# K and Q of the first half batch in fp32 by SyncE's queue, in a fused attention and feed-forward kernel

## The chip, the cores and the metric

The kernel runs on one core of one Trainium2 chip. The core has five engines that work side by side and wait for each other by semaphores: TensorE (PE, matrix products), VectorE (DVE), ScalarE (ACT), GpSimd (POOL) and SyncE (SP). Sixteen DMA engines move data between HBM and the on-chip memory; transfers are issued from the queues of SyncE, ScalarE or GpSimd. In this kernel a transfer that changes the type (fp32 in HBM, fp16 on chip) is always issued from GpSimd.

The metric is the device time of one execution in microseconds. The kernel before took 384.3 us (median of three runs, 384.25 to 387.24).

## The reference

Attention over 8 batches, 12 heads, 448 tokens and head size 64, and a feed-forward layer with SiLU on its result:

```python
scores = (1 / sqrt(64)) * q @ k.transpose(0, 1, 3, 2)
attn = exp(scores - max(scores)) ; attn = attn / (sum(attn) + 1e-09)
x = (attn @ v).transpose(0, 2, 1, 3).reshape(3584, 768)
h = x @ w_in                      # 768 x 2048
out = (h * sigmoid(h)) @ w_out    # 2048 x 768, fp32
```

q, k, v and the weights come in fp32.

## The kernel before

**Tiling.** Heads go in three groups of four, so that a tile holds 4 heads x 32 rows on its 128 partitions, with 14 tokens of 64 numbers on each. A *unit* is the work of one batch, one head group and a range of queries. Batch 0 is cut into two pieces of 224 queries, so units 0, 1, 2 are its first half for the three head groups and units 3, 4, 5 its second; from unit 6 on a unit has all 448 queries. K of a head group of batch 0 is loaded whole with its first unit; Q is loaded by unit.

**A unit's path.** K and Q arrive in fp16 (`load_k`, `load_q`, GpSimd's queue, which casts), VectorE transposes them in 32 x 32 blocks (`turn_k`, `turn_q`, lines 411 and 422), PE multiplies them into scores (`score`, L430), ScalarE takes exponentials out of PSUM into the tiles E (`expo`, L469), PE sums them (L510, L524) and multiplies them by V (L495), VectorE inverts the sums and scales into xT (L634). In the first half of the kernel the feed-forward part follows each batch: `ffn1` (L647), tanh on ScalarE (L668), the gate on VectorE (L693), and products with w_out in a seven-product scheme (L864; the first 256 tokens in the plain way, L877) whose results go through the `ost` tiles to HBM (`store`, L912). The last two pairs of batches use a similar scheme for w_in (L783).

**Score bursts.** For the first `TILED` units (3), two chunks of keys are scored in one burst, and every third burst is cut into two halves of two heads each; the halves use two PSUM banks, whole bursts four. Later units use three banks and one.

**The first loads.** Q of unit 0 is an exception: `first_q` (L342) loads it in fp32 on SyncE's queue into a T buffer that is idle then, and ScalarE casts it (`cast_q`, L347). All else comes by GpSimd's queue in the order of `LOADS`, where `u` is a unit's K and Q (Q alone where K is there), `v0` is V of all of batch 0, `v3` V of batch 1's first head group, `i` a quarter of w_in and `o` a quarter of w_out. At most eight of GpSimd's loads are in flight.

**What sets the order.** The order of instructions on PE, ACT and DVE is worked out when the kernel is built: the class `Order` plays the work through with an assumed cost for each step (`act`, `mm`, `DMA_RATE`, `DMA_PAUSES`) and starts what is ready, by biases such as `READ_B` or `GATE_B`. Then the instructions are written out in that order, and each engine runs its list in order whatever the real times are. Where the plan expects PE to wait in the first part, it puts multiplications of zeros there (`run_zeros`, L1815), so that PE does not fall idle; their number of columns is part of the program. An opening block of `FIRST` x 128 columns and a little more comes ahead of the first scores. All constants below `EAGER` are inputs of that plan, and a change to any of them redraws the order.

**The end.** The last quad of row tiles ends with product 2; `take_last` copies its result out of PSUM in two halves, one on VectorE (L929) and one on ScalarE (L930), into one tile, and `store` writes it in four stores of 32 rows, by turns on SyncE's and ScalarE's queue.

Of the kernel before, what the change touches and what calls it, by code (L numbers as in the profile page):

```python
# [35 lines left out]
def act(n):  # L36
    return n * 0.000824 + 0.177
# [61 lines left out]
class Order:  # L99


    def __init__(self, shy, nice):
        self.now, self.shy, self.nice = 0.0, shy, nice
        self.free = {"PE": 1.0, "ACT": 2.1, "DVE": 1.2, "POOL": 1.2}
# [55 lines left out]
    def load(self, rows, row_bytes, emit, ring=None):  # L160
# [6 lines left out]
        self.pool.append((op, took, ring, lane, begin))  # L167
        return op

    def step(self):  # L170

        soon = []
        for eng in ("ACT", "DVE"):
            if self.free[eng] > self.now:
                soon.append(self.free[eng])
                continue
            best, urgent = None, None
            for op in self.wait[eng]:
                at = op.ready()
                if at is None:  # L180
                    continue
                if at > self.now:
                    soon.append(at)
                    if op.bias <= -10 and (urgent is None or at < urgent):
                        urgent = at
# [35 lines left out]
def kernel(  # L221
# [9 lines left out]
    nc = tc.nc  # L231
# [46 lines left out]
    LOOK = 1  # L278
    SOON = -5
    KEEP = 0  # L280
# [45 lines left out]
    def group_of(src, b, hg):  # L326
        return src[b, HG * hg : HG * (hg + 1)].rearrange("h (i g) d -> (h i) (g d)", g=TPP)
# [3 lines left out]
        nc.gpsimd.dma_start(out=t, in_=group_of(k, b, hg))  # L331
        rawk[(b, hg)] = t

    def stage(name):
        t = sb.tile([128, HG, S], FP16, name=name, tag="T", bufs=NT_)
        return t.rearrange("p h s -> p (h s)").bitcast(FP32)

    first_in = {}

    def first_q():  # L340
        first_in["q"] = stage("first_q")[:, 0 : D * units[0][3]]
        nc.sync.dma_start(out=first_in["q"], in_=group_of(q, 0, 0)[:, 0 : D * units[0][3]])  # L342
        q_tile[(0, 0)] = sb.tile([128, TPP * D], FP16, name="rq_0_0", tag="rq", bufs=NRQ)
        rawq[0] = q_tile[(0, 0)][:, 0 : D * units[0][3]]

    def cast_q():
        nc.scalar.copy(out=rawq[0], in_=first_in["q"])  # L347

    def load_q(n):
        b, hg, g0, g1 = units[n]  # L350
# [539 lines left out]
    def bank(qd, m):  # L890
        return pr_t[(qd, m)][:, 0:OH]
# [30 lines left out]

    def take_2(qd):
        nc.scalar.copy(out=ost(qd, 0, 0), in_=bank(qd, 1))
        store(qd, 0, 0)

    def take_last(qd):
        t, mid = ost(qd, 0, 0), OH // 2
        nc.vector.tensor_copy(out=t[:, 0:mid], in_=bank(qd, 1)[:, 0:mid])  # L929
        nc.scalar.copy(out=t[:, mid:OH], in_=bank(qd, 1)[:, mid:OH])  # L930
        store(qd, 0, 0)

    def take_6(qd):
# [66 lines left out]
    def plan_first():  # L1000
        t_ring.take()
        rq_ring.take()
        q_in = Op("SP", 0.0, first_q)
        od.emit(q_in.emit)
        q_in.done = FIRST_Q
        ld_q[0] = od.add(
            Op("ACT", act(D * units[0][3]), cast_q, [q_in], -4, tail=0.25, then=t_ring.give)
        )

    def plan(what):  # L1010
        kind, at = what[0], int(what[1:])
        if kind == "u":
            b, hg = units[at][:2]
            if at < NG or b:
                plan_k(b, hg)
            if at:
                plan_q(at)
            else:
                plan_first()
# [382 lines left out]
    def queue_quad(qd):  # L1402
# [16 lines left out]
        def queue(m):  # L1419
            def run():  # L1420
# [506 lines left out]
```

## Time and profile before

| | |
|---|---|
| median of three runs | 384.3 us |
| the profiled execution, own time | 384.07 us |
| its span, first to last instruction | 382.3 us |
| PE busy in the span | 375.4 us (98%), 5528 matmuls |
| DVE, ACT, POOL busy | 296.3, 243.2, 87.5 us |
| zeros on PE | 44 matmuls, 1.2 to 20.8 us |
| first scores on PE (L430) | 6.71 us |
| last product on PE starts, last copy ends | 377.8 us, 378.9 us |
| GpSimd's DMA queue / SyncE's | 22.70 MB / 10.47 MB |

A busy PE is not a PE at work on scores: zeros count as busy, and so do matmuls at a low clock. Times within the timeline are counted from the span's start. In a row of the timeline, `x12` is a number of instructions put together, and the bracket tells how long the engine was idle before and what released it. K, Q, V and the weights of one load are given in the size that lands on chip: a K load of 224 KB in fp16 reads 448 KB of fp32.

### The profile page before, as it was taken

The page shows a single profiled execution, that of the slowest core. Times are in us where ns is not written, and L with a number is a line of the kernel's source. Part 1 is how long each engine was busy: PE and PEld are TensorE (multiplying, and loading weights), DVE is VectorE, ACT ScalarE, POOL GpSimd, SP SyncE. Part 2 cuts the span into 40 slices and gives each one's busy share as a digit, 9 for nine tenths or more (in the row PEclk, how much of TensorE's full clock was granted, in tenths as well). Part 3 has the DMA queues.
Part 4 walks back from the last instruction along what each step waited for, and adds up shares of the span by engine and source line. Part 5 has one row for each costly group of instructions (what it writes and reads, how often), then busy time and mean ns, then how long its engine had stood idle before and what let it go on. Part 6 is the DMA issues. An engine that isn't in the chain of part 4 may idle for free.

```text
span 382.3 us, 12926 instructions
## 1 busy us (share of the span) xinstructions
PE 375.4 (98%) x5528; PEld 197.9 (52%) x5528; DVE 296.3 (77%) x549; ACT 243.2 (64%) x378; POOL 87.5 (23%) x158
## 2 busy tenths in 40 slices
PE   8999999999999999999999999999999999999995
PEld 3667665444444444445444445555556655556663
DVE  3566676998979988897988789898899557777652
ACT  4988894788977488976487868128770138871010
POOL 7745354603306064233153200000000000000000
PEclk9999999999999999999999999999999999999999
DMA  8999999852829493729292500320002330001333
GB/s 136 199 206 205 209 151 196 147 94 26 123 50 133 104 159 47 121 43 157 70 184 38 76 9 19 79 69 0 2 0 58 94 99 2 0 2 45 103 102 83
DMA packets 37225, 34.77 MB, mean 91 GB/s; under 512 B 11696, under 2 KB 37168, under 8 KB 37168
## 3 DMA queue, kind: packets, MB, share of 16 engines
q0 software_dynamic: 26272, 22.70, 39.9%
q1 hardware_dynamic: 10128, 10.47, 10.2%
q10 hardware_dynamic: 768, 0.79, 0.8%
q8 instruction: 43, 0.70, 0.8%
q14 instruction: 14, 0.11, 0.1%
HBM read 45.61 MB, written 11.01 MB: 148 GB/s over the span
## 4 chain that ended last, share of the span: by engine, by line
PE 95%; DMA 2%; DVE 1%; ACT 1%; issue 0%; ACTq 0%; POOLq 0%
PE P L864 31%; PE P L647 20%; PE P L783 17%; PE P L430 11%; PE P L495 10%; PE P L877 3%; PE P L510 2%; DMA rk<-in_k_dram 1%; PE P L1815 1%; ACT E L469 1%; PE P L524 1%; DMA out_dram<-ost 0%; DVE xT L634 0%; DVE KT L411 0%; DVE G L693 0%
## 5 line engine op out<-in xcount | busy, mean ns | idle before, releaser
L469 ACT ACTIVATE E<-P 128x448 f16<-128x448 f32 (+6 forms) x168 | 151.2, 936 | 46.4 <-PE P L430 45.0
L647 PE MATMUL P<-xT,w_in_t 128*32 128x448 f16 (+1 forms) x1344 | 82.2, 340 | 0.0
L376 POOL DMA_DIRECT2D V<-in_v_dram x84 | 46.2, 565 | 91.0 <-PE P L495 77.1
L647 PEld LDWEIGHTS <-w_in_t 128*32 128x32 f16 (+1 forms) x1344 | 45.5, 97 | 33.9 <-issue 14.5
L864 PEld LDWEIGHTS <-G 128*32 128x32 f16 (+1 forms) x976 | 39.3, 97 | 29.2 <-issue 6.5
L430 PE MATMUL P<-rq,KT 32*128 32x448 f16 (+4 forms) x864 | 50.9, 340 | 1.0 <-DVE KT L411 0.6
L693 DVE SCALAR_TENSOR_TENSOR G<-G,P 128x448 f16<-128x448 f16 x64 | 38.6, 609 | 12.3 <-ACT G L668 11.4
L864 PEld LDWEIGHTS <-S 128*32 128x32 f16 (+1 forms) x720 | 30.8, 97 | 22.0 <-issue 3.8
L864 PE MATMUL P<-w_out_t,S 128*32 128x384 f16 (+1 forms) x472 | 39.1, 327 | 0.0
L864 PE MATMUL P<-D,G 128*32 128x384 f16 (+1 forms) x496 | 38.8, 327 | 0.0
L668 ACT ACTIVATE G<-P 128x448 f16<-128x448 f32 x64 | 35.0, 549 | 2.2 <-PE P L647 1.3
L864 PE MATMUL P<-w_out_t,G 128*32 128x384 f16 (+1 forms) x480 | 35.9, 327 | 0.0
L495 PE MATMUL P<-E,V 128*32 128x448 f16 (+2 forms) x672 | 34.3, 355 | 0.5 <-DVE xT L634 0.5
L917 DVE TENSOR_TENSOR ost<-P,u 128x384 f32<-128x384 f32 x39 | 21.5, 550 | 15.6 <-PE P L864 9.0
L783 PE MATMUL P<-sx,tw 128*128 128x448 f16 x144 | 29.9, 352 | 0.0
L634 DVE SCALAR_TENSOR_TENSOR xT<-P,R 128x448 f16<-128x448 f32 x42 | 24.3, 617 | 6.3 <-PE P L495 3.2
L430 PEld LDWEIGHTS <-KT 32*128 32x128 f16 (+2 forms) x864 | 14.4, 98 | 27.7 <-issue 23.4
L783 PEld LDWEIGHTS <-tw 128*128 128x128 f16 x192 | 18.8, 98 | 17.5
L495 PEld LDWEIGHTS <-V 128*32 128x32 f16 (+2 forms) x672 | 14.8, 95 | 18.5 <-issue 10.5
L480 DVE TENSOR_TENSOR T<-T,E 128x1792 f16<-128x1792 f16 x20 | 21.5, 1077 | 1.3 <-ACT E L469 1.2
L569 DVE STREAM_TRANSPOSE R<-P 128x448 f32<-128x448 f32 (+1 forms) x17 | 10.8, 636 | 15.1 <-PE P L510 7.4
L480 DVE TENSOR_TENSOR T<-E,E 128x1792 f16<-128x1792 f16 x20 | 21.6, 1080 | 0.1
(83 smaller groups left out, 439.6 us busy)
## 6 DMA issues: line engine op xcount, KB each, us to landing
out_dram<-ost SPq DMA_DIRECT2D x208, 48.0 KB, 1.6
rk<-in_k_dram POOLq DMA_DIRECT2D x24, 224.0 KB, 5.3
rq<-in_q_dram POOLq DMA_DIRECT2D x21, 224.0 KB, 5.8
w_in_t<-in_moe_w_in_dram POOLq DMA_DIRECT2D x12, 256.0 KB, 8.5
w_out_t<-in_moe_w_out_dram POOLq DMA_DIRECT2D x4, 768.0 KB, 10.4
V<-in_v_dram POOLq DMA_DIRECT2D x43, 64.0 KB, 4.2
V<-in_v_dram POOLq DMA_DIRECT2D x40, 48.0 KB, 4.5
out_dram<-ost ACTq DMA_DIRECT2D x16, 48.0 KB, 1.8
```

What stands on the lines that cost most here:

```text
L376: nc.gpsimd.dma_start(out=VT[(b, hg0)][32 * x : 32 * (x + 1), :, 0:count, :], in_=v[b, hs].rearrange("h (i g) d -> i h g d", g=TPP)[:, :, ...
L430: nc.tensor.matmul(out=P[p0 : p0 + 32 * (x1 - x0), pS[h], at : at + nq], lhsT=KT[(b, hg)][32 * h : 32 * (h + 1), c, x0:x1, :, e], rhs=QT[n ...
L469: nc.scalar.activation(out=E[(n, w)][0:kr, h0:h1, 0:nk], in_=P[0:kr, bank : bank + h1 - h0, 0:nk], func=AF.Exp, scale=attn_scale,)
L480: nc.vector.tensor_tensor(out=T[n], in0=T[n] if step else E[(n, 0)], in1=E[(n, step + 1)], op=ALU.add,)
L495: nc.tensor.matmul(out=a[32 * h : 32 * (h + 1), 0:nq], lhsT=w, rhs=e[k0:k1, h, at : at + nq], start=start, stop=stop, skip_group_check=True,)
L634: nc.vector.scalar_tensor_tensor(out=xc(b, cc)[:, 32 * g0 : 32 * g1], in0=acc[(n, part)][:, 0:nq], scalar=0.5, in1=rdn_t[n].rearrange("p g ...
L647: nc.tensor.matmul(out=h_t[(b, f, t0)][m0:m1, 0 : t1 - t0], lhsT=w_in_t[:, cc, 128 * f + m0 : 128 * f + m1], rhs=xc(b, cc)[:, t0:t1], star ...
L668: nc.scalar.activation(out=g, in_=h, func=AF.Tanh)
L693: nc.vector.scalar_tensor_tensor(out=g, in0=g, scalar=1.0, in1=h, op0=ALU.add, op1=ALU.mult)
L783: nc.tensor.matmul(out=pp_t[(*key, PBANK[m])], lhsT=w[:, c, :], rhs=xc(pb + x[0], 3 * x[1] + c) if isinstance(x, tuple) else sx_t[(pb, x)] ...
L864: nc.tensor.matmul(out=pr_t[(qd, BANK[m])][m0:m1, 0:OH], lhsT=w[:, f, m0:m1], rhs=W_[m][:, f, :], start=(f == 0 and BANK[m] == m), stop=(f ...
L917: nc.vector.tensor_tensor(out=out, in0=a, in1=b, op=op)
```

## The change

K of head groups 0, 1 and 2 of batch 0 and Q of units 0, 1 and 2 are loaded in fp32 by six DMAs of SyncE's queue, in the order K0, Q0, K1, Q1, K2, Q2, into T and E buffers that are not yet in use. VectorE casts the first 9 of 14 tokens of K0, and all of K1, K2, Q1 and Q2; ScalarE casts the rest of K0 and Q0. GpSimd's queue begins with Q of unit 3, V of batch 1's first head group and V of batch 0.

The constants of the plan change: among others `TILED` from 3 to 5, `FIRST` from 40 to 47, `WHOLE` from 7 to 10 and `HOLD` from 0 to 0.8. The order on PE, ACT and DVE is another one up to about 300 us; the products after that stand in the same order. At the end `take_last` is gone, one ScalarE copy takes its place, and one store of the tile before goes to SyncE instead of ScalarE.

```diff
-FIRST_Q = 3.5
-DMA_PAUSES = ((0.0, 0.4), (4.0, 1.35), (15.5, 0.9), (21.0, 0.7), (48.5, 0.8), (65.0, 0.8))
+FAST_ISSUE, FAST_START, FAST_TAIL, FAST_RATE = 0.42, 1.25, 0.9, 430000.0
+DMA_PAUSES = ((15.5, 0.9), (21.0, 0.7), (48.5, 0.8), (65.0, 0.8))
...
+    def fast(self, rows, row_bytes, emit):
+        op = Op("SP", FAST_ISSUE, emit)
+        self.fast_loads.append((op, rows * row_bytes / FAST_RATE))
+        return op
...
-    NEAR = 0.1
-    LATE = -2.0
+    NEAR = 0.25
+    LATE = -1.0
     COLD = 8.5
-    FIRST = 40
-    WHOLE = 7
-    TANH_B = -1
-    GATE_B = -6
+    FIRST = 47
+    WHOLE = 10
+    TANH_B = -2
+    GATE_B = -1
     ADD_B = 1
-    SUM_B = -3
+    SUM_B = -1
     COPY_B = -1
-    READ_B = -2
-    PAIR_B = -2
-    SILU_B = -2
-    HOLD = 0
+    READ_B = -3
+    PAIR_B = -6
+    SILU_B = -0.3
+    HOLD = 0.8
...
-    TILED = 3
+    TILED = 5
...
-    LOADS = "u0 u1 u2 v0 u4 u3 i0 i3 u5 i2 u6 o0 v3 i1 u7 o1 u8 o2 v4 v5 o3"
-    TURN = 8
+    LOADS = "u0 u3 u1 v3 u2 v0 u5 u4 i1 i2 u6 i0 o2 o0 u8 i3 u7 o1 v4 v5 o3"
+    TURN = 12
...
+    def first_k(hg):
+        t = stage("k0", "T", NT_) if hg == 0 else stage(f"k{hg}", "E", NE)
+        nc.sync.dma_start(out=t, in_=group_of(k, 0, hg))
+        rawk[(0, hg)] = sb.tile([128, TPP * D], FP16, name=f"rk_0_{hg}", tag="rk", bufs=NRK)
+
+    def first_q(n):
+        c1 = D * units[n][3]
+        t = stage("q0", "T", NT_) if n == 0 else stage("q", "E", NE)
+        first_in["q", n] = t = t[:, 0:c1] if n < 2 else t[:, c1 : 2 * c1]
+        nc.sync.dma_start(out=t, in_=group_of(q, 0, n)[:, 0:c1])
...
+    def cast_k(hg, i0, i1, eng):
+        part = slice(D * i0, D * i1)
+        eng(out=rawk[(0, hg)][:, part], in_=first_in[f"k{hg}"][:, part])
+
+    def cast_q(n, eng):
+        eng(out=rawq[n], in_=first_in["q", n])
...
-            eng = nc.scalar if w % 2 and 4 * qd + 8 >= NT * B else nc.sync
+            last = w == 1 if (qd, i, j) == (NT * B // 4 - 1, 0, 1) else w % 2
+            eng = nc.scalar if last and 4 * qd + 8 >= NT * B else nc.sync
...
-    def take_last(qd):
-        t, mid = ost(qd, 0, 0), OH // 2
-        nc.vector.tensor_copy(out=t[:, 0:mid], in_=bank(qd, 1)[:, 0:mid])
-        nc.scalar.copy(out=t[:, mid:OH], in_=bank(qd, 1)[:, mid:OH])
-        store(qd, 0, 0)
...
-                elif m == 2 and final:
-                    ost_ring.give(od.now)
-                    od.add(Op("DVE", 0.35, lambda: take_last(qd), [op], -20))
```

More of the change, by code (lines that the diff above doesn't have):

```diff
@@ L103, in __init__ @@
         self.now, self.shy, self.nice = 0.0, shy, nice
-        self.free = {"PE": 1.0, "ACT": 2.1, "DVE": 1.2, "POOL": 1.2}
+        self.fast_loads = []
+        self.free = {"SP": 0.74, "PE": 1.0, "ACT": 2.1, "DVE": 1.2, "POOL": 1.2}
         self.wait = {"ACT": [], "DVE": []}
@@ L168, in load @@
         return op
+    def fast(self, rows, row_bytes, emit):
+        op = Op("SP", FAST_ISSUE, emit)
+        self.fast_loads.append((op, rows * row_bytes / FAST_RATE))
+        return op
     def step(self):
         soon = []
+        if self.free["SP"] > self.now:
+            soon.append(self.free["SP"])
+        elif self.fast_loads:
+            op, took = self.fast_loads.pop(0)
+            self.start(op)
+            self.dma_free = max(self.dma_free, self.now + FAST_START) + took
+            op.done = self.dma_free + FAST_TAIL
+            soon.append(self.free["SP"])
         for eng in ("ACT", "DVE"):
@@ L332, in load_k, with stage @@
         rawk[(b, hg)] = t
-    def stage(name):
-        t = sb.tile([128, HG, S], FP16, name=name, tag="T", bufs=NT_)
-        return t.rearrange("p h s -> p (h s)").bitcast(FP32)
     first_in = {}
[L340 to L347, printed above, removed]
+    def stage(what, tag, bufs):
+        if what not in first_in:
+            t = sb.tile([128, HG, S], FP16, name=f"fp32_{what}", tag=tag, bufs=bufs)
+            first_in[what] = t.rearrange("p h s -> p (h s)").bitcast(FP32)
+        return first_in[what]
+    def first_k(hg):
[7 more added lines that the diff above has]
+        nc.sync.dma_start(out=t, in_=group_of(q, 0, n)[:, 0:c1])
+        q_tile[(0, n)] = sb.tile([128, TPP * D], FP16, name=f"rq_0_{n}", tag="rq", bufs=NRQ)
+        rawq[n] = q_tile[(0, n)][:, 0:c1]
+    def cast_k(hg, i0, i1, eng):
[3 more added lines that the diff above has]
+        eng(out=rawq[n], in_=first_in["q", n])
     def load_q(n):
@@ L999, with plan_first @@
     NB0 = NG * len(PIECES)
-    def plan_first():
-        t_ring.take()
+    def plan_first(n):
+        rk_ring.take()
         rq_ring.take()
[L1003 to L1008, printed above, removed]
+        nq = D * units[n][3]
+        k_in = od.fast(128, 4 * TPP * D, lambda: first_k(n))
+        q_in = od.fast(128, 4 * nq, lambda: first_q(n))
+        ring = t_ring if n == 0 else e_ring
+        if n < 2:
+            ring.take(2)
+        vec, sca = nc.vector.tensor_copy, nc.scalar.copy
+        if n == 0:
+            ld_k[(0, 0)] = [
+                od.add(Op("DVE", 0.49, lambda: cast_k(0, 0, 9, vec), [k_in], -5)),
+                od.add(
+                    Op(
+                        "ACT",
+                        act(5 * D),
+                        lambda: cast_k(0, 9, TPP, sca),
+                        [k_in],
+                        -5,
+                        tail=0.25,
+                        then=ring.give,
+                    )
+                ),
+            ]
+            ld_q[0] = od.add(
+                Op("ACT", act(nq), lambda: cast_q(0, sca), [q_in], -5, tail=0.25, then=ring.give)
+            )
+            return
+        if n == 2:
+            ring.take()
+        ld_k[(0, n)] = [
+            od.add(Op("DVE", 0.75, lambda: cast_k(n, 0, TPP, vec), [k_in], TURN, then=ring.give))
+        ]
+        then = ring.give if n == 2 else None
+        ld_q[n] = od.add(Op("DVE", 0.39, lambda: cast_q(n, vec), [q_in], TURN, then=then))
     def plan(what):
@@ L1013, in plan @@
             b, hg = units[at][:2]
-            if at < NG or b:
+            if at < NG:
+                plan_first(at)
+                return
+            if b:
                 plan_k(b, hg)
[L1016 to L1019, printed above, removed]
+            plan_q(at)
         elif kind == "v":
```

## The prediction

> **What bounds the kernel now.** I read the page's chain of waits first, then the table of stretches, then the timeline of the first 25 us and of the last 6, burst by burst. The chain says whose queue ends last:
>
> ```profile
> PE 95%; DMA 2%; DVE 1%; ACT 1%; issue 0%; ACTq 0%; POOLq 0%
> ```
>
> The stretches (length, then busy us of PE, PEld, DVE, ACT, POOL, the granted clock, the DMA share, GB/s written) say where PE has room:
>
> ```profile
> 0.00:5.00 5.00, 3.81 (x9) 1.35 (x10) 1.04 (x8) 1.85 (x2) 3.96 (x11) 1.00 0.59 99
> 5.00:10.00 5.00, 4.12 (x53) 2.23 (x55) 2.55 (x8) 2.67 (x3) 3.21 (x6) 1.00 1.18 178
> 10.00:15.00 5.00, 5.00 (x79) 2.53 (x75) 2.44 (x7) 4.96 (x5) 4.14 (x7) 1.00 1.38 196
> 40.00:45.00 5.00, 5.00 (x64) 3.52 (x65) 2.99 (x7) 4.28 (x8) 1.09 (x3) 1.00 1.15 209
> 150.00:200.00 50.00, 50.00 (x1060) 23.58 (x1052) 43.06 (x74) 37.61 (x52) 18.69 (x35) 1.00 0.69 112
> ```
>
> PE is full from 10 us on, but not with work: up to 21 us part of it is multiplications of zeros that the order of work puts where it expects PE to wait. ScalarE is the full engine at 10 to 15 us (4.96 of 5). DMA writes 196 to 209 GB/s of fp16, so reads about 400 GB/s of fp32. Hence the change can act on three things: the time of the first scores, the filler behind them, and the end. The timeline of the start (start, busy, engine):
>
> ```profile
> 1.19 4.88 PE L1815 MATMUL P<-zeros 128*128 128x512 f16 x12 [1.19 <-DVE cols L306]
> 3.35 0.56 ACT L347 CAST rq<-first_q 128x448 f16<-128x448 f32 x1 [1.34 <-DMA first_q<-in_q_dram]
> 5.95 0.70 DVE L411 STREAM_TRANSPOSE KT<-rk 128x384 f32<-128x384 f32 x2 [1.58 <-DMA rk<-in_k_dram]
> 6.71 0.97 PE L430 MATMUL P<-rq,KT 32*128 32x224 f16 x24 [0.64 <-DVE KT L411]
> 7.33 4.82 ACT L469 ACTIVATE E<-P 128x896 f16<-128x896 f32 x4 [3.41 <-PE P L430]
> ...
> 12.37 0.58 PE L430 MATMUL P<-rq,KT 32*128 32x224 f16 x16
> 12.88 0.45 PE L1815 MATMUL P<-zeros 128*128 128x384 f16 x2
> 13.26 0.60 PE L430 MATMUL P<-rq,KT 32*96 32x224 f16 x8
> 13.79 1.10 PE L1815 MATMUL P<-zeros 128*128 128x512 f16 x8
> 14.82 0.60 PE L430 MATMUL P<-rq,KT 32*96 32x224 f16 x16
> ```
>
> The reader is to see that the first scores wait for K (loaded 1.24 to 5.9 us), and the prices: a whole score burst takes 0.51 us from its start to the next (12.37 to 12.88), a half one of only two heads 0.53 (13.26 to 13.79), and 2,176 filler columns with a change of kind of burst 1.03 (13.79 to 14.82); with about 0.10 for the change, 0.427 ns a column. Before 6 us a column costs twice that: 5,632 columns fill 1.19 to 5.86. The end:
>
> ```profile
> 376.89 0.56 DVE L917 TENSOR_TENSOR ost<-P,u 128x384 f32<-128x384 f32 x1 [0.74 <-DMA out_dram<-ost]
> 378.19 0.36 DVE L929 COPY ost<-P 128x192 f32<-128x192 f32 x1 [0.74 <-DMA out_dram<-ost]
> 378.58 0.32 ACT L930 COPY ost<-P 128x192 f32<-128x192 f32 x1 [9.01 <-DVE ost L929]
> ```
>
> The two halves of the last copy run one after the other: ScalarE's waits for VectorE's.
>
> **The change part by part.** All sums are against the profiled execution, 384.07 us (span 382.3 and 1.8 around it), 0.2 under the median of 384.3.
>
> *First scores.* The opening filler grows from 5,632 to 6,016 columns. At the early rate (0.83 ns) it ends at 6.18, so scores can start at 6.28 instead of 6.71: 0.43 gained. PE's rate doubles somewhere between 5.86 and 6.71, since the burst at 6.71 already runs at the fast rate; if it does so only at 6.7, half of the gain is lost in the slow first burst. I take -0.2 (bounds 0 and -0.43).
>
> Can K and Q be there? The one fp32 load on SyncE's queue, 224 KB, landed 2.6 us after its issue at 0.74. K0 is twice that: another 224 KB at 400 GB/s is 0.56, so it lands at 3.9, Q0 at 4.5. Behind it stand the casts, which no row shows. VectorE's bounds: 0.60 ns an element (the 1,792-element fp16 add in 1.08) and 1.26 (ScalarE's cast row, 448 in 0.565); I take 0.84, between them, since it is one operand in fp32. K0: 0.5 on VectorE beside ScalarE's 0.44 (320 elements, between its 0.32 for 192 and 0.565 for 448); transpose 0.70; Q0's cast 0.565 from 4.5; its transpose 0.41. That is ready at 5.5, or 6.1 with every load half a microsecond late: the filler decides. ScalarE's share lies in the 3.41 us in which it waited for its first scores; VectorE's five casts, 3,264 elements or 2.0 to 4.1 us, lie in the 6.4 us that it had idle before 10 us. Without that cover they would be paid whole.
>
> *Filler behind the first scores.* 9,856 columns become 7,808: 2,048 x 0.427 = -0.87. These are instructions in PE's program, not a forecast: what remains is paid whether the data are early or not, which limits the gain.
>
> *More bursts.* TILED goes from 3 to 5, and the instruction order shows four bursts cut in halves instead of two: 2 x (0.53 + 0.53 - 0.51) = +1.10. Beyond these, PE's list changes between score, strip and full-width bursts 195 times after the opening instead of 189; two of the six are in the prices above, four at 0.11 add +0.44. All other PE work is the same list of products reordered (12 w_out products go from strips to full width: 0.17 and 0.163 us each, nothing). ScalarE has two exponentials fewer (16 to 14 for units 0 to 4), about 0.18 each from 0.92 against 1.67 for double the size: -0.36 on an engine that bounds only up to 17 us.
>
> *Waits that are not filler.* Six gaps on PE in this run exceed an ordinary change: 0.14 at 7.9, 0.23 at 9.3, 0.18 at 23.6, 0.20 at 24.8, and 0.30 each at 89.9 and 146.8, 1.35 in all. A redrawn order removes some and makes others, and no row shows which. From below, all go (-1.35); from above, they stay and new ones come (next part). With the exponentials ahead I take half: -0.65.
>
> *Who must be on time.* Adding the same prices along the new order of PE's list from 6.5: unit 1's scores at 9.4 (9.84 before), unit 2's at 12.0 (12.37), V of batch 0 first used at 14.1 (16.07). In order of arrival K1 lands at 5.6, K2 at 7.3, each later by what GpSimd's queue moves ahead of them, 0.56 for the fourth unit's Q and some of batch 1's V: 6.2 and 8.4. On VectorE 2.7 us stand between K1's landing and unit 1 (cast 0.75, transposes 0.70, Q1's cast 0.4, two Q transposes 0.82), and 2.3 for unit 2, so the limits are 6.7 and 9.7. That holds, K1 with half a microsecond. GpSimd's queue loses five loads (three K, two Q), and V moves ahead of the weights. Q3 and all of V end after 4.1 MB of fp32; before, they ended after 3.4 MB with the fourth V load landing at 13.5. Another 0.7 MB is 1.75 us, the earlier start of SyncE's queue gives back about 0.9: 14.3, at the need.
>
> [...] A row bears on whether a queue waits behind another:
>
> ```profile
> out_dram<-ost SPq DMA_DIRECT2D x10, 48.0 KB, 4.2
> out_dram<-ost SPq DMA_DIRECT2D x208, 48.0 KB, 1.6
> ```
>
> Ten stores of SyncE between 60 and 70 us, with GpSimd's loads in flight, took 4.2 us, against 1.6 over all; the packets of the first did not move for two microseconds while GpSimd's backlog did. This looks like order of arrival, and SyncE's six loads, issued first, then go ahead. [...]
>
> *The end.* One ScalarE copy of 384 columns (0.48 in the same line's rows) replaces 0.36 and 0.32 in sequence with a gap, 378.19 to 378.90: -0.22. SyncE gets a third store of the tile before, each about 0.42 after the last, which brings its next to 378.75: -0.15 is left.
>
> Sum: -0.2 - 0.87 + 1.10 + 0.44 - 0.65 - 0.15 = -0.33, so 383.7. Its own bounds: -1.35 (every wait gone, full early rate) and +0.4 (all waits stay): 382.7 to 384.5.
>
> **The rivals.** *SyncE's and GpSimd's loads share evenly* (slower). From 2.8 us each queue gets 200 GB/s. Of the 1,120 KB to the end of K1, 200 are through by then, the rest takes 4.6: K1 at about 7.9, unit 1 ready at 10.6, 1.2 late; K2 and Q2 end at 12.3, unit 2 ready 1.5 later, 0.6 beyond that. ScalarE, full there, and everything behind it move by 1.8: 385.5. It decides if K1 lands after 6.7. For: GpSimd's first packets move at 2.8 us, before four of the six fp32 loads. Against: the slow stores. [...]
>
> *VectorE's casts hold up GpSimd* (slower). If GpSimd cannot issue while the casts of K0 and K1 run, its last load of batch 0's V, at about 6.6 by its rows of 0.57 and 0.65, comes at 7.9 and, with the 7.2 us that these loads took, lands at 15.1: 1.0 late, 384.7. Against: in this trace GpSimd's issues took the same 0.55 to 0.57 us with VectorE busy throughout as without. But that VectorE work is transposes and fp16 adds, not such casts. [...]
>
> *The loads gain nothing* (the change does not do what it says): the same 16 engines already read 400 GB/s, so K0 comes earlier but everything behind comes when it did. Then the early waits stay and half bursts are paid: the upper bound, 384.5.
>
> **How the numbers follow.** Forecast 0.5 (383.7, own range 382.7 to 384.5); even sharing 0.2 (385.5); held-up GpSimd 0.1 (384.7); nothing gained 0.15 (384.5); 0.05 for a new wait in the middle that no row shows. The range: at the bottom the lower bound with another 0.5 for casts and clock, 382.2; at the top even sharing with the held-up queue on it, 386.6. One per cent, about what a measurement tells from no change, is 3.8 us. Faster by that cannot come from 1.35 us of waits and 0.87 of filler: 0.03. Slower by it needs both slow rivals and a further wait: 0.07. Within: 0.90.
>
> **What would show it.** Right: first scores near 6.3 and unit 1's at 9.4; filler behind them of 7,808 columns with little idle time; K1 landed by 6.7; VectorE not waited for by PE at unit 2; last copy 0.48 long. Wrong: PE waiting on VectorE's casts or transposes at units 1 and 2 (even sharing), on V at 14 us (held-up GpSimd), or PE gaps after 25 us that this run lacks.

## The result and the profile after

The changed kernel takes 389.68 us (median of four runs, 388.09 to 391.18) against 384.27 us of the kernel before on the same chip: a ratio of 1.0138, 95% interval 1.0107 to 1.0168. It is 5.4 us slower. The profiled execution took 388.09 us, with a span of 386.3 us against 382.3.

The page's chain of waits, whose line of before said PE 95%, DMA 2%:

```profile
PE 93%; DMA 5%; DVE 1%; issue 0%; ACT 0%; SPq 0%; DVEq 0%; ACTq 0%; POOLq 0%
```

The chain's pieces in order of time (start us, us, what) begin with

```profile
1.25 7.05 DMA rq<-in_q_dram
8.59 8.74 DMA G<-in_v_dram
```

Up to 17.3 us the time is set by two loads of GpSimd's queue, Q of unit 3 and, behind it, the fourth V load of batch 0. The same stretches as before (length, busy us of PE, PEld, DVE, ACT, POOL, the granted clock, which is the share of its full rate that PE is recorded to run at, the DMA share, GB/s written):

```profile
0.00:5.00 5.00, 3.81 (x9) 1.35 (x10) 1.34 (x9) 2.04 (x3) 3.96 (x11) 1.00 0.65 185
5.00:10.00 5.00, 4.53 (x45) 2.11 (x43) 2.21 (x7) 3.21 (x4) 2.27 (x4) 1.00 1.06 273
10.00:15.00 5.00, 3.12 (x54) 1.55 (x54) 3.18 (x9) 2.79 (x3) 2.63 (x5) 1.00 1.55 194
40.00:45.00 5.00, 5.00 (x56) 4.46 (x54) 3.32 (x7) 4.72 (x8) 2.64 (x5) 1.00 1.21 205
150.00:200.00 50.00, 50.00 (x1052) 23.52 (x1048) 43.33 (x72) 36.49 (x50) 17.75 (x33) 1.00 0.57 91
```

PE was full from 10 to 15 us before, now it is busy 3.12 of 5.00. GB/s counts what is written on chip: up to 10 us much of it is fp32 that is written as it was read, so 273 is no higher rate of reading than the 178 of before (the DMA view below gives 295 GB/s read). The timeline of the start (start, busy, engine; the bracket is the idle time and what ended it):

```profile
4.18 0.46 DVE L371 CAST rk<-fp_k 128x576 f16<-128x576 f32 x1 [2.45 <-DMA fp_k<-in_k_dram]
...
6.32 1.09 PE L457 MATMUL P<-rq,KT 32*128 32x224 f16 x24
...
8.51 0.63 DVE L371 CAST rk<-fp_k 128x896 f16<-128x896 f32 x1 [2.76 <-DMA fp_k<-in_k_dram]
...
8.59 0.78 POOL L403 DMA_DIRECT2D G<-in_v_dram  x1 [2.51 <-DMA rq<-in_q_dram]
...
10.82 0.58 PE L457 MATMUL P<-rq,KT 32*128 32x224 f16 x16 [1.22 <-DVE rq L449]
...
11.52 0.63 DVE L371 CAST rk<-fp_k 128x896 f16<-128x896 f32 x1 [0.76 <-DMA fp_k<-in_k_dram]
...
14.57 0.57 PE L457 MATMUL P<-rq,KT 32*128 32x224 f16 x16 [1.06 <-DVE rq L449]
...
17.37 0.57 PE L522 MATMUL P<-E,G 128*32 128x224 f16 x16 [0.70 <-DMA G<-in_v_dram]
...
22.12 0.57 PE L522 MATMUL P<-E,cols 128*32 128x224 f16 x16 [0.21 <-DVE xT L661]
...
25.86 0.71 PE L522 MATMUL P<-E,G 128*32 128x224 f16 x16 [0.18 <-DVE R L596]
...
31.30 0.57 PE L522 MATMUL P<-E,G 128*32 128x224 f16 x16 [0.77 <-DVE G L720]
```

The reader is to see three waits for loads (K1 is cast only at 8.51 and unit 1 starts at 10.82; K2 at 11.52, unit 2 at 14.57; V at 17.37) and three later ones, for other engines. The end:

```profile
381.21 0.56 DVE L945 TENSOR_TENSOR ost<-P,u 128x384 f32<-128x384 f32 x1 [0.74 <-DMA out_dram<-ost]
382.51 0.48 ACT L952 COPY ost<-P 128x384 f32<-128x384 f32 x1 [8.44 <-DMA out_dram<-ost]
```

Following the two lists of PE's work side by side with the row prices of the prediction, the difference of the two profiled executions comes out so (a wait is counted as what a gap exceeds an ordinary start of the next burst, so unit 1's bracket of 1.22 counts 1.29):

| term | predicted | measured |
|---|---|---|
| first scores (6.71 to 6.32) | -0.20 | -0.39 |
| filler behind them, 7,808 columns for 9,856 | -0.87 | -0.87 |
| half bursts and changes of kind | +1.54 | +1.46 |
| waits that are not filler (1.37 to 5.17) | -0.65 | +3.80 |
| the end, from PE's last group to the end of the span (5.60 to 5.31) | -0.15 | -0.29 |
| sum | -0.33 | +3.7 (span +4.0) |

The 0.3 us between the sum and the span belong to no term. Of the 5.17 us of waits 3.19 are at units 1 and 2 and at V (1.29, 1.13, 0.77), and 1.63 at 22.1, 25.9, 26.5 and 31.3 us (0.28, 0.25, 0.14, 0.96). The rest of the median's 5.4 us is not in this execution; the eighth experiment finds it.

### The profile page after: what moved, and what is told of

Read it like the earlier page. It is cut to its first block, busy times and chain, and to the rows that moved or that the text cites. A ratio compares the mean times of both kernels' runs of the same rounds, so it can differ in the third digit from the quotient of the medians.

```text
span 386.3 us, 12823 instructions
## 1 busy us (share of the span) xinstructions
PE 376.9 (98%) x5483; PEld 197.5 (51%) x5483; DVE 299.3 (77%) x541; ACT 244.3 (63%) x377; POOL 85.1 (22%) x153
## 4 chain that ended last, share of the span: by engine, by line
PE 93%; DMA 5%; DVE 1%; issue 0%; ACT 0%; SPq 0%; DVEq 0%; ACTq 0%; POOLq 0%
PE P L891 31%; PE P L674 20%; PE P L810 16%; PE P L457 11%; PE P L522 10%; PE P L904 3%; DMA G<-in_v_dram 2%; DMA rq<-in_q_dram 2%; PE P L537 2%; PE P L551 1%; DMA out_dram<-ost 0%; DVE R L596 0%; DVE G L720 0%; DVE ost L945 0%; ACT R L837 0%
## 5 line engine op out<-in xcount | busy, mean ns | idle before, releaser
L674 PEld LDWEIGHTS <-w_in_t 128*32 128x32 f16 (+1 forms) x1344 | 45.8, 97 | 33.0 <-issue 13.6
L457 PE MATMUL P<-rq,KT 32*128 32x448 f16 (+4 forms) x864 | 52.0, 340 | 2.4 <-DVE rq L449 2.3
L720 DVE SCALAR_TENSOR_TENSOR G<-G,P 128x448 f16<-128x448 f16 x64 | 38.6, 610 | 13.6 <-ACT G L695 12.5
L457 PEld LDWEIGHTS <-KT 32*128 32x128 f16 (+2 forms) x864 | 15.2, 99 | 30.1 <-issue 24.7
L661 DVE SCALAR_TENSOR_TENSOR xT<-P,R 128x448 f16<-128x448 f32 x42 | 24.3, 619 | 5.2 <-PE P L522 4.3
L949 ACT COPY u<-P 128x384 f32<-128x384 f32 x13 | 6.3, 483 | 26.0 <-PE P L891 21.1
```

The lines of the kernel that those rows point to most:

```text
L457: nc.tensor.matmul(out=P[p0 : p0 + 32 * (x1 - x0), pS[h], at : at + nq], lhsT=KT[(b, hg)][32 * h : 32 * (h + 1), c, x0:x1, :, e], rhs=QT[n ...
L661: nc.vector.scalar_tensor_tensor(out=xc(b, cc)[:, 32 * g0 : 32 * g1], in0=acc[(n, part)][:, 0:nq], scalar=0.5, in1=rdn_t[n].rearrange("p g ...
L674: nc.tensor.matmul(out=h_t[(b, f, t0)][m0:m1, 0 : t1 - t0], lhsT=w_in_t[:, cc, 128 * f + m0 : 128 * f + m1], rhs=xc(b, cc)[:, t0:t1], star ...
L720: nc.vector.scalar_tensor_tensor(out=g, in0=g, scalar=1.0, in1=h, op0=ALU.add, op1=ALU.mult)
```

## The experiments

Theory S: SyncE's and GpSimd's loads share the DMA engines, so K1 and K2 come late (S1: shared with GpSimd's queue; S2: SyncE's own loads advance side by side). Rival O: the redrawn order costs by itself. Rival C: VectorE's casts hold up GpSimd. Kernels built from the changed one keep its end.

**The constants alone.** The kernel before, its loads and its `LOADS`, with the new constants:

```diff
-    FIRST = 40
+    FIRST = 47
...
-    TILED = 3
+    TILED = 5
...
-    HOLD = 0
+    HOLD = 0.8
```

> The kernel before with the changed constants of the plan (NEAR, LATE, FIRST, WHOLE, TANH_B, GATE_B, SUM_B, READ_B, PAIR_B, SILU_B, HOLD, TILED, TURN), but its old loads and old list LOADS. Theory S (the DMA engines alternate between SyncE's and GpSimd's packets, so K1, K2 and then V come late): the loads are as before, so the time stays within 1 us of before, 383.5 to 385.5. Rival O (the redrawn order itself costs: half bursts, more changes, tighter gates): 386.5 to 388.5. Rival C (VectorE's fp32 casts hold GpSimd's issues): as S, since there are no such casts.

Measured: 385.87 against 383.92 us, ratio 1.0050 (1.0035 to 1.0065). That lies between the ranges of S and O: the new constants cost about two microseconds without any of the new loads. In the timeline of this kernel two of the waits above stand already, with the same lengths, though its loads are the old ones:

```profile
19.13 0.57 PE L495 MATMUL P<-E,cols 128*32 128x224 f16 x16 [0.21 <-DVE xT L634]
...
22.87 0.97 PE L495 MATMUL P<-E,G 128*32 128x224 f16 x16 [0.18 <-DVE R L569]
```

**The loads alone.** The changed kernel with the constants and `LOADS` of before; the six fp32 loads, their casts and the plan's `DMA_PAUSES` stay:

```diff
-    FIRST = 47
+    FIRST = 40
...
-    LOADS = "u0 u3 u1 v3 u2 v0 u5 u4 i1 i2 u6 i0 o2 o0 u8 i3 u7 o1 v4 v5 o3"
+    LOADS = "u0 u1 u2 v0 u4 u3 i0 i3 u5 i2 u6 o0 v3 i1 u7 o1 u8 o2 v4 v5 o3"
```

> The changed kernel with the constants and the list LOADS of the kernel before (TILED 3, FIRST 40 and so on); the six fp32 loads, the casts and the new end stay, the order is redrawn by the plan. S1 and S2: K1 and K2 land late again (8 us and 11 us), waits of about 1 us each for units 1 and 2, little after 20 us: 385.0 to 387.0. O: with the old constants the loss goes, 383.0 to 384.5.

Measured: 387.58 against 383.90 us, ratio 1.0104 (1.0076 to 1.0131). O's range is out, and S's top of 387.0 was too low. K1 is late here too, now with V of batch 0 at the head of GpSimd's queue instead of unit 3's Q and V of batch 1:

```profile
8.62 0.63 DVE L371 CAST rk<-fp_k 128x896 f16<-128x896 f32 x1 [2.80 <-DMA fp_k<-in_k_dram]
...
10.76 0.58 PE L457 MATMUL P<-rq,KT 32*128 32x224 f16 x16 [1.82 <-DVE rq L449]
```

The loads cost 3.7 us and the constants 2.0, together 5.6 against the 5.4 of the whole change, which agrees within the intervals. It is no exact split: each kernel has an order and a filler of its own (6,784 columns behind the first scores with the constants alone, 10,752 here), and the new list `LOADS` is in neither.

**V of batch 1 behind the rest.** GpSimd's first loads in another order: V of batch 0, Q of units 3, 5, 4, six of w_in, then V of batch 1.

```diff
+    turn = list(range(5, 9)) + [0, 9, 10] + list(range(11, 17)) + list(range(1, 5))
+    moved = [od.out[od.slots[i]][2] for i in turn]
+    for i, fn in enumerate(moved):
+        od.out[od.slots[i]] = (*od.out[od.slots[i]][:2], fn)
```

> The changed kernel with GpSimd's list alone reordered, all other engines' lists unchanged: V of batch 0 first, then the Q loads, six weight loads, and V of batch 1 last of these. S: K1 and K2 still share with V, so unit 1's scores stay near 10.8 us and unit 2's near 14.5; but the fourth V load no longer waits for the first Q load to land, V of batch 0 is there by 14 to 15 instead of 17.3 and the 0.77 us wait before its first use goes: 0.5 to 1.2 us faster than the changed kernel, 387.0 to 387.6 against 388.1. O: no change, 388. C: no change or slower.

Measured: 396.64 against 383.92 us, ratio 1.0348 (1.0320 to 1.0377). This was a badly chosen edit: Q of unit 3 now lands at 16.3, and VectorE's list has its transpose ahead of unit 1's. PE stands 7.8 us for it. It says nothing for or against S; it shows what a load that nobody needs yet does when its transpose stands early in a list that is run in order. K1 was at 9.43.

**GpSimd held until K1 has landed.** A one-column copy of K1 stands at the head of GpSimd's list:

```diff
+    for i in od.sp_slots:
+        od.out[i][2]()
+    nc.gpsimd.tensor_copy(out=held[:, 0:1], in_=first_in["k1"][:, 0:1])
...
```

> The changed kernel with one GpSimd copy of a single column of the fp32 K1 ahead of its first load, so that GpSimd's queue starts only when K1 has landed; all else the same. S: K1 lands at 5.5 to 6.0 instead of 8.4 and K2 at 7 to 8 instead of 11.5, unit 1's scores start by 9.6 and unit 2's by 12.2, both waits of 1.1 to 1.3 us go; V of batch 0 starts 4 us later and PE then waits 1 to 2.5 us for it: 386 to 387.5. O: K1 may come earlier but the time stays near 388. C: the casts of K1 and K2 now fall in GpSimd's issues, which get longer than 0.8 us, V comes after 18 us: 388.5 or more.

Measured: 390.01 against 383.92 us, ratio 1.0159 (1.0144 to 1.0174); the time again says little, since Q of unit 3 lands at 11.19 and unit 1 stands behind its transpose. It lies in C's range, but not for C's reason: GpSimd's issues took 0.54 to 0.70 us each, not more than 0.8. The measurement is K1's landing with SyncE's queue alone:

```profile
7.59 0.63 DVE L375 CAST rk<-fp_k 128x896 f16<-128x896 f32 x1 [1.84 <-DMA fp_k<-in_k_dram]
```

0.9 us earlier than in the changed kernel, and 2.0 later than the forecast of 5.6. So sharing with GpSimd's queue (S1) is the smaller part of the delay. The DMA view of the changed kernel, 4.5 to 8.5 us (queue: packets, MB, share of 16 engines):

```profile
q1 hardware_dynamic: 331, 0.88, 67.8%
q0 software_dynamic: 295, 0.15, 29.6%
```

and the same view of this kernel:

```profile
q1 hardware_dynamic: 523, 1.23, 85.4%
```

q1 is SyncE's queue, q0 GpSimd's. With both at work they move about the same number of packets, 331 and 295, and SyncE's rate falls from 308 to 220 GB/s (1.23 and 0.88 MB in 4 us). In these 4 us neither goes ahead of the other. In bytes they are far apart: GpSimd's 0.15 MB of fp16 are 0.30 MB read, a third of SyncE's. By the same view of single microseconds SyncE's and GpSimd's packets are 95 and 100 from 6 to 7 us, 94 and 95 from 7 to 8, 101 and 101 from 8 to 9; before and after they are not even (48 and 91 from 4 to 5, 43 and 333 from 10 to 11). How an engine picks between the queues is not shown.

**Unit 3's Q first, then held.** As the last, but Q of unit 3 is issued at once, and V of batch 0 stands ahead of batch 1's behind the hold.

```diff
+    turn = [0] + list(range(5, 9)) + [9, 10] + list(range(11, 17)) + list(range(1, 5))
...
+    def hold_then(fn):
+        nc.gpsimd.tensor_copy(out=held[:, 0:1], in_=first_in["k1"][:, 0:1])
+        fn()
...
+    moved[1] = lambda fn=moved[1]: hold_then(fn)
```

> The changed kernel with GpSimd's list alone reordered: first the Q load of unit 3 (whose transpose stands on VectorE ahead of unit 1's), then the one-column copy that waits for K1, then V of batch 0, two Q loads, six weight loads, V of batch 1. Three theories for the lateness: S1, sharing with GpSimd's queue; S2, the loads of SyncE's own queue progress side by side, so that K1 lands only when much of Q1 and K2 has moved too, whatever GpSimd does; O, the redrawn order. S1: K1 by 6.5 us, unit 1's scores by 9.5, 385.0 to 386.0. S2: K1 at 7.5 to 8.0 as in the held run before, unit 1's scores at 10.0 to 10.4, unit 2's by 12.9, V of batch 0 at 14.5 to 16: 386 to 387.5. O: the gaps on PE after 20 us (0.28, 0.25, 0.14, 0.96) are all there in either case.

Measured: 389.62 against 383.90 us, ratio 1.0146 (1.0117 to 1.0175), outside the ranges of S1 and S2. K1 at 8.36, unit 1 at 10.68:

```profile
8.36 0.63 DVE L375 CAST rk<-fp_k 128x896 f16<-128x896 f32 x1 [2.67 <-DMA fp_k<-in_k_dram]
```

With one load on the other queue (224 KB of fp32 read), issued at 1.25 us, K1 lands at 8.36 instead of 7.59; V behind it adds little (8.51 in the changed kernel, 8.79 in its second profile, so 0.3 is not resolved). The waits after 20 us are there as O said: 0.21, 0.18 and 0.77 us of idle PE at 22.96, 26.70 and 31.99.

**K2 and Q2 only after K0's cast.** GpSimd held as before, and SyncE's last two loads issued from 4.85 us on, into K0's fp32 buffer (lines against the kernel of "GpSimd held"):

```diff
-    for i in od.sp_slots:
+    for i in od.sp_slots[:4]:
...
+        if casts["n"] == 2:
+            casts["n"] = 9
+            first_in["k2"] = first_in["k0"]
+            for j in od.sp_slots[4:]:
+                od.out[j][2]()
```

> The changed kernel with GpSimd's queue held until K1 has landed, and K2 and Q2 issued only when K0 has been cast, about 4.7 us, into K0's buffer; for the landing of K1 alone, the time does not matter. S2: with K2 and Q2 out of the way K1 lands at 5.6 to 6.5 us, against 7.6 with them. S1 or a slow start of this queue: 7.2 to 7.6 as before.

Measured, in one execution of 391.73 us:

```profile
7.20 0.63 DVE L378 CAST rk<-fp_k 128x896 f16<-128x896 f32 x1 [1.32 <-DMA fp_k<-in_k_dram]
```

K1 at 7.20 misses S2's 5.6 to 6.5 and stands at the edge of the rival's 7.2 to 7.6. But Q1 and, from 4.85 us, K2 were still on the queue, so this kernel does not decide between the two.

**K1 with nothing behind it.** Only K0, Q0 and K1 at the start; K2, Q1 and Q2 when K1 is cast (lines against the kernel just above):

```diff
-        casts["n"] += hg == 0
+        casts["n"] += 1
...
-    for i in od.sp_slots[:4]:
+    for i in od.sp_slots[:3]:
...
-        if casts["n"] == 2:
+        if casts["n"] == 3:
...
-            first_in["k2"] = first_in["k0"]
-            for j in od.sp_slots[4:]:
+            first_in["k2"] = first_in["k1"]
+            for j in [od.sp_slots[j] for j in (4, 3, 5)]:
```

> As e9_k2_after_k0, but only K0, Q0 and K1 (1,120 KB) are issued at the start; K2, Q1 and Q2 follow on SyncE's queue when K1 is cast (K2 goes into K1's fp32 buffer), and GpSimd's queue is held until K1 has landed. Nothing is in flight beside K1 but K0 and Q0. Unit 1 and all behind it come late by construction; only K1's landing (start of its cast) is measured. In e9 and e3 SyncE's queue had moved 1,120 KB by about 5.8 us by its packets, yet K1 landed at 7.20 and 7.59. Theory S2 (loads of one queue advance side by side, so that Q1, and K2, take from K1): K1 lands at 6.2 to 6.7. Rival U (K1 is slow by itself: the queue's own pace and its last packets): K1 at 7.0 or later.

Measured, in the timeline of this kernel (one execution, 390.5 us, unit 1 late as built):

```profile
4.00 0.46 DVE L378 CAST rk<-fp_k 128x576 f16<-128x576 f32 x1 [2.26 <-DMA fp_k<-in_k_dram]
...
6.21 0.63 DVE L378 CAST rk<-fp_k 128x896 f16<-128x896 f32 x1 [0.63 <-DMA fp_k<-in_k_dram]
```

K1 lands at 6.21, in S2's range; U's 7.0 is out. 672 KB from K0's landing to K1's took 2.21 us, 311 GB/s. So the loads that SyncE issues *behind* K1 delay it: 6.21 without them, 7.20 with Q1 and a later K2 and Q2, 7.59 with all three from the start.

But the delay is not spread over the whole load, as S2 would have it of loads side by side. The trace also records the sixteen counts with which each load reports its landing; K1's cast starts 0.02 to 0.03 us after the last. K1's counts, in us:

| kernel | eighth | twelfth | thirteenth | last |
|---|---|---|---|---|
| K1 with nothing behind it | 5.68 | 5.83 | 5.98 | 6.18 |
| GpSimd held, Q1 behind K1, K2 and Q2 from 4.85 us on | 5.90 | 6.28 | 6.41 | 7.17 |
| GpSimd held, Q1, K2 and Q2 behind K1 | 5.60 | 5.99 | 6.01 | 7.57 |
| unit 3's Q first, then held | 6.56 | 7.61 | 7.68 | 8.34 |
| the changed kernel | 6.45 | 6.93 | 8.18 | 8.48 |

With GpSimd's queue idle, the thirteenth count comes at 5.98 to 6.41, whatever stands behind K1 on its own queue, and the last one at 6.18 to 7.57: the delay lies mostly in the last three. With GpSimd's queue at work the eighth comes later too. Each row is one execution.

**The changed kernel again.** No edit; to see the executions whose clock was lower.

> The changed kernel once more, nothing edited. The sum over its profiled execution (span 386.3, granted clock 0.999) has waits of 1.29 at 10.82, 1.13 at 14.57 and 0.77 at 17.37 us; its executions of 390.96 and 391.18 us had a mean clock of 0.987. Theory H (a part of the loss is PE at half clock after the gaps that late loads leave): an execution near 391 shows the waits of unit 1 or 2 at 1.9 us or more and a stretch of half granted clock of 3.4 us or a multiple of it right behind, before 25 us, and the rest as in the profiled run of 388.1. Rival R (something else in those executions): the clock lost is elsewhere in the span, or the waits are the same as in the run of 388.1.

Measured: 389.84 against 384.33 us (387.37 to 393.05), ratio 1.0137 (1.0085 to 1.0189). The profiled execution took 391.83 us. In its timeline:

```profile
8.79 0.63 DVE L371 CAST rk<-fp_k 128x896 f16<-128x896 f32 x1 [3.03 <-DMA fp_k<-in_k_dram]
...
11.10 0.58 PE L457 MATMUL P<-rq,KT 32*128 32x224 f16 x16 [2.13 <-DVE rq L449]
```

and its stretches, where the granted clock is the third number from the right (0.50 is half the full rate):

```profile
10.00:12.00 2.00, 0.90 (x18) 0.43 (x18) 1.22 (x6) 0.27 (x1) 0.54 (x1) 0.99 1.39 224
12.00:14.00 2.00, 2.00 (x18) 0.88 (x18) 1.19 (x3) 2.00 (x2) 0.90 (x2) 0.50 1.52 191
...
22.00:24.00 2.00, 2.00 (x34) 1.08 (x36) 0.86 (x3) 1.05 (x2) 0.94 (x2) 0.50 1.22 186
24.00:26.00 2.00, 2.00 (x40) 1.08 (x32) 1.35 (x4) 1.27 (x1) 0.74 (x1) 0.60 1.14 183
```

H holds in this execution. PE reached its full clock earlier here (at 5.13 instead of 6.63 us, by the trace's record of the clock), so the opening filler ended earlier (first scores at 5.82 instead of 6.32); K1 came a little later, so the same gap in front of unit 1 is 2.13 us long instead of 1.22; from 0.85 us after its end PE runs at half clock for 13.6 us, and the span is 3.7 us longer. PE looks full in those stretches (2.00 of 2.00): only the clock column tells. Of eight executions of the changed kernel, four had a mean clock of 0.996 or more and took 387.4 to 388.4 us, four 0.982 to 0.987 and 391.0 to 393.1; this is what the median holds beyond the first profile, as far as one profile of the four longer executions can show it.

**The plan told the truth.** One constant, so that the plan expects K1 at 8.5 and K2 at 11.9 us:

```diff
-FAST_ISSUE, FAST_START, FAST_TAIL, FAST_RATE = 0.42, 1.25, 0.9, 430000.0
+FAST_ISSUE, FAST_START, FAST_TAIL, FAST_RATE = 0.42, 1.25, 0.9, 204000.0
```

> The changed kernel, with one constant of the plan set so that it expects what the trace shows: FAST_RATE 204000 instead of 430000 puts K1 at 8.5 and K2 at 11.9 us. The loads and casts are the same; the plan fills PE with 264 more instructions in the list of the opening part. Theory L (the loss is that the data are late): the waits at units 1 and 2 turn into filler, PE has no gap of 1.9 us and no half clock, and the profiled run stays near that of the changed kernel, 387 to 388.5, the median with it. Theory P (the loss is that the plan was wrong about the data, and PE could do other work in the time): the waits go and nothing comes for them, 385 to 386.

Measured: 390.32 against 384.33 us (389.37 to 390.75), ratio 1.0157 (1.0142 to 1.0172), the clock at 0.999 or more in all four. In its timeline

```profile
8.64 1.97 PE L1861 MATMUL P<-zeros 128*128 128x512 f16 x13
11.03 0.97 PE L457 MATMUL P<-rq,KT 32*128 32x224 f16 x24 [0.42 <-DVE rq L449]
...
12.43 3.60 PE L1861 MATMUL P<-zeros 128*128 128x512 f16 x25
```

zeros stand where the waits were (17,856 columns behind the first scores instead of 7,808), and with them the half clock is gone. P falls: the plan, told when the data come, found no other work for PE. L is right on the waits, but its number was too low, 390.2 for 387 to 388.5 in the profiled run: the 10,048 more columns cost 4.3 us at 0.427 ns, more than the 3.2 us of waits whose place they take. This plan starts unit 2 at 15.96, 1.4 later than the changed kernel, and it has waits of its own at 27.6 and 33.5 us.

**K1, Q1, K2, Q2 by GpSimd, in fp16, first in its list.** The new order stays; the casts of these four fall away:

```diff
+        if hg:
+            nc.gpsimd.dma_start(out=rawk[(0, hg)], in_=group_of(k, 0, hg))
+        else:
+            nc.sync.dma_start(out=t, in_=group_of(k, 0, hg))
...
```

> The changed kernel with K1, Q1, K2, Q2 undone: in fp16 by GpSimd's queue at the head of its list, without the four VectorE casts; K0 and Q0 stay on SyncE's queue; all other lists unchanged. S: only K0 and Q0 are shared, K1 lands at 6.3 to 7.2, unit 1's scores start by 9.6 and unit 2's by 12.3; V of batch 0 comes after 4.1 MB at about 15, a wait near 1 us: 385.5 to 387. O: near 388 as the order is the same. C: GpSimd's issues at their 0.55 to 0.67 us, 386 to 387 also, so this run does not part C from S.

Measured: 387.48 against 383.92 us, ratio 1.0119 (1.0062 to 1.0177), between the ranges of S and O; the profiled execution, 386.94, lies in S's.

```profile
6.69 0.70 DVE L450 STREAM_TRANSPOSE KT<-rk 128x384 f32<-128x384 f32 x2 [0.94 <-DMA rk<-in_k_dram]
...
29.98 0.57 PE L534 MATMUL P<-E,G 128*32 128x224 f16 x16 [0.77 <-DVE G L732]
```

K1 at 6.69, 1.8 us earlier than in the changed kernel. What remains: unit 1 is still 0.81 late at 10.44, behind a pair of Q transposes on VectorE that waited for a Q load until 9.68 (the profile puts the wait down to ScalarE's exponentials, which came last); V is late by 0.74 at 15.83; and the order's waits stand at 20.6, 24.3, 25.0 and 30.0 us. The last of them, 0.77 us of idle PE, is the one at 31.30 in the changed kernel, unchanged although K1 and K2 are early.

**K0 and Q0 alone in fp32.** The constants, `LOADS` and pauses of before, the new end, and the others by GpSimd in the old places:

```diff
-            if at < NG:
+            if at == 0:
                 plan_first(at)
                 return
-            if b:
+            if at < NG or b:
                 plan_k(b, hg)
```

> As the run with old constants, but only K0 and Q0 come in fp32 by SyncE's queue; K1, Q1, K2, Q2 in fp16 at the head of GpSimd's queue without VectorE casts. S1 and S2: the first scores start at 6.2 to 6.4 instead of 6.7, K1 lands by 6.9 as in the earlier run with these loads, no wait for units 1 and 2 above 0.3 us: 383.0 to 384.0, as fast as the kernel before or up to 0.9 us faster. O: the same. If the early start of SyncE's loads only delays GpSimd's: 384.5 to 386.

Measured: 384.08 against 383.90 us over ten runs (383.66 to 384.61), ratio 1.0003 (0.9994 to 1.0012): no difference, at the upper edge of the range of S1 and S2.

```profile
5.63 0.97 PE L457 MATMUL P<-rq,KT 32*128 32x224 f16 x24 [0.37 <-DVE rq L449]
...
7.04 0.71 DVE L438 STREAM_TRANSPOSE KT<-rk 128x384 f32<-128x384 f32 x2 [1.47 <-DMA rk<-in_k_dram]
...
8.75 0.58 PE L457 MATMUL P<-rq,KT 32*128 32x224 f16 x16 [0.16 <-ACT E L496]
```

First scores come 1.1 us earlier than in the profile of before, in part by chance, since PE had its full clock at 4.18 us here and at 6.75 there. K1 lands at 7.04 with nothing ahead of it on its queue, and unit 1 waits for ScalarE, not for K1. The gain is not seen in the total: the plan fills 10,176 columns here (320 more, 0.14 us) and has 0.4 us more of other waits; the rest was not followed up.

**The end alone.** The kernel before with one ScalarE copy instead of `take_last`, and the third store on SyncE:

```diff
-            eng = nc.scalar if w % 2 and 4 * qd + 8 >= NT * B else nc.sync
+            last = w == 1 if (qd, i, j) == (NT * B // 4 - 1, 0, 1) else w % 2
+            eng = nc.scalar if last and 4 * qd + 8 >= NT * B else nc.sync
...
-                elif m == 2 and final:
-                    ost_ring.give(od.now)
-                    od.add(Op("DVE", 0.35, lambda: take_last(qd), [op], -20))
```

> The kernel before with the new end alone: take_last gone, one ScalarE copy in its place, one store of the tile before on SyncE instead of ScalarE. The prediction's term: 0.15 faster than before (0.22 of the copy less the store), ratio 0.9996; rival: the store that SyncE takes over lies on the path and takes it back or more, 1.000 or above. In both the last copy is one row of about 0.48 us.

Measured: 383.97 against 384.33 us (twelve and seventeen runs), ratio 0.9999 (0.9976 to 1.0021): a term of 0.15 is below what this tells. The row is as forecast:

```profile
377.89 0.48 ACT L925 COPY ost<-P 128x384 f32<-128x384 f32 x1 [8.62 <-DMA out_dram<-ost]
```

From the start of PE's last group to the end of the last copy it is 1.98 us (376.39 to 378.37) instead of 2.21 (376.69 to 378.90). To the end of the span, though, it is 5.62 instead of 5.60 here, and 5.31 in the changed kernel: whether the 0.2 us of the copy reach the end is not resolved. No version here beats the kernel before by more than its interval.

## Why the prediction was wrong

The forecast was "no change, 383.7", 0.90 within one per cent; the kernel became 1.4% slower, outside the range.

- **The step that failed** is "Who must be on time": "In order of arrival K1 lands at 5.6, K2 at 7.3", and with GpSimd's loads 6.2 and 8.4, inside the limits of 6.7 and 9.7. They landed at 8.51 and 11.52. The runs take the 2.9 us from 5.6 to 8.5 apart, each by one profiled execution. 0.6 are there with K1 alone (6.21): K0 landed 0.1 later than summed, and from there SyncE's fp32 loads moved 311 GB/s, not the 400 read off GpSimd's casting loads. 1.4 come with the loads behind K1 on its own queue (7.20, 7.59), mostly in its last three counts. 0.8 come with unit 3's Q on the other queue (8.36), and 0.15 remain. The single steps are uncertain: two kernels with loads of the same sizes at the head of both queues (the loads alone, and V of batch 1 behind the rest) had K1 at 8.62 and 9.43. The two groups are clear: K1 landed between 6.21 and 7.59 in the three kernels in which GpSimd's queue had nothing until then, and between 8.36 and 9.43 in the six profiles in which it had a load from the start.
- **The reading behind it** was that ten stores that took 4.2 us against 1.6 show order of arrival. They show that a transfer can be slow while another queue is at work; they do not show who goes first. In these runs the sum in order of arrival put K1 too early even with GpSimd's queue idle: 5.6 for 6.21, 7.20 and 7.59.
- **V** was put at 14.3 for a need of 14.1, and landed at 17.33. No more than eight of GpSimd's loads were in flight: eight were issued by 6.1 us, Q of unit 3 came back only at 8.30, and the fourth V load, 2.51 us late, went into the same crowd and took 8.74 where it took 7.3 before. The limit stood in the description of the kernel and was not used in the sum. It is the smaller part: in the second profile this load was issued at 7.40, 1.2 us earlier, and still landed at 16.76.
- **Waits that are not filler**, "I take half: -0.65", with an upper bound of what before had: measured +3.80. 1.6 of it lies behind 22 us, and two of these waits stand with the same length in the kernel that has the new constants alone. The largest, 0.77 us of idle PE, does not stand there, but it stands with that length in the kernels that keep the changed order with other loads. The case "a new wait in the middle that no row shows" had 0.05 in the forecast, though a redrawn order has no reason to be free of them.
- **Even sharing**, the rival at 0.2, named the right point of decision ("if K1 lands after 6.7") and came near: K1 at 7.9, unit 1 at 10.6 were forecast, 8.51 and 10.82 measured. Half of it was right, that the queues share: 331 and 295 packets in the same 4 us. Its 200 GB/s for each queue were not: SyncE's kept 220, GpSimd's read 75. The delay by SyncE's own later loads was not in it, and its sum as written, 2.8 and 4.6 us, gives 7.4, not 7.9; that it came near is in part luck. Its price of 1.8 us was too low: 2.4 at units 1 and 2, 0.8 at V, and the half clock behind such gaps, which no case had.
- **Held-up GpSimd**, that GpSimd cannot issue while VectorE casts, was the author's supposition, and no run shows it: of the two issues that stand beside the casts of K1 and Q1, one took 0.78 instead of some 0.64, the other 0.69 instead of 0.55. Its effect on the time was not tried apart from the rest. VectorE's casts were cheaper than taken, 576 elements in 0.46 and 896 in 0.63 us.
- **Right** were the terms that were counted in PE's list: filler (-0.87), half bursts and changes (1.54 for 1.46), the length of the last copy. The first scores, at 6.32 for a forecast of 6.28, were right by luck: PE had its full clock at 6.63 us there, and in the second profile of the same kernel, with the full clock at 5.13, they stood at 5.82.
- **Small slips in the sum**, which change nothing above: with every wait gone and the full early rate the terms add to -1.26, not -1.35, and the two gaps put at 89.9 and 146.8 us end at 90.75 and 147.63 in the trace.

## What to carry to other kernels

Do not price a load by the bytes that were issued before it: here what was issued behind it on the same queue put off its last parts (K1 at 6.21 us with nothing behind it, at 7.59 with three loads), and what another queue moved took from it as well (8.36 for 7.59 with one load there), so issue late what is needed late, and measure one load's landing before a chain is built on it. A redrawn order needs a charge of its own for new waits, and it can be run alone, without the change that came with it. After every gap on PE in the start look at the granted clock of the microseconds behind it, since a PE at half clock counts as busy (2.00 us of 2.00 at a clock of 0.50). The very start is an exception: the column reads 1.00 for the first 5 us of both kernels, where a column of zeros costs 0.83 ns, twice 0.427.

## What the runs showed of the hardware

- K1 was delayed by later loads of its own queue: its landing went from 6.21 to 7.20 and 7.59 us as more was issued behind it. The thirteenth of its sixteen counts came at 5.98, 6.41 and 6.01, so the delay is mostly in the last three. There are sixteen DMA engines too, but the trace does not say which engine a packet or a count belongs to, so why some parts lag stays open.
- Around a gap of 2.13 us PE's clock was halved for about 13.6 us (from 11.95 to 25.6) although PE was busy all that time; behind one of 1.22 us it was not. By the traces' record of the clock the same holds in six other kernels here: gaps of 1.78, 1.82, 2.83, 2.99, 4.21 and 7.77 us came with stretches of half clock of 6.8, 3.4, 10.2, 6.8, 6.8 and 10.2 us, and no profile whose longest gap was 1.22 us or less has one while PE works. The stretch does not grow with the gap. All seven lie at one to four times 3.4 us; what sets that length is not shown.
